# Unmixed weight blocks fetched raw, split at first use and written back once, with five plain half-experts

## The chip, the cores and the metric

The kernel runs on one core of a Trainium2 chip. The metric is the device time of one execution in microseconds (us). Besides the plain runs there is one profiled execution, whose trace gives all the rows below. TensorE (PE) multiplies, VectorE (DVE), ScalarE (ACT) and GpSimd (POOL) work on the results and on the weights, and SyncE (SP) issues nearly all DMA transfers.

## The reference

Three steps are chained: attention with a window of 64 positions over 32 heads of 576 positions, a dense layer pair with ELU, and eight experts whose outputs are weighted by a matrix P that is normalised by rows and columns in eight rounds. The change touches the last one alone:

```python
N, D, E, F = (2304, 512, 8, 1024)
...
out = np.zeros((N, D), dtype=np.float32)
for e in range(E):
    h = np.maximum(x @ w1[e], 0.0)
    ye = h @ w2[e]
    out += P[:, e:e + 1] * ye
```

## The kernel before, in words

Every float32 operand is split in two parts: a high part, rounded to the type that TensorE multiplies fast (`R32`), and a low part, the rest. A product of two operands is three matmuls: high by high, high by low, low by high. ScalarE makes the high part with a copy, and VectorE or GpSimd makes the low part with a subtraction.

The 2304 tokens are three groups of 768. An expert's 1024 hidden features are two **half-experts** of 512, so there are 16. A half-expert can be done in two ways.

- **Plain** (`e_in`, `e_out`, matmul lines L932 to L934 and L950 to L952): the first `PU` half-experts of group 0 run so, in units, with the weights' high and low parts held in SBUF as `forms` (tiles f). One unit has 96 matmuls of the first layer, half of them 512 and half 256 columns wide, and 72 of the second with 512 columns.
- **Block products** (`l1` and `l2`): all others, in **periods** of one half-expert each. Operands are cut into 2 x 2 blocks, and seven products of blocks, or of sums of blocks, take the place of eight. A period has 14 calls of `l1` (seven products for each of two halves p, six matmuls of 384 columns each, L1127) and seven calls of `l2` (18 matmuls of 256 columns in group 0, L1272, and 12 of 384 in the others, L1207). The loop goes in steps s of two `l1` calls and one `l2` call. `l2` follows `LAG` = 8 steps behind, so the first steps have `l1` calls alone.

A block product needs seven weight blocks of each matrix, split in high and low: three that are blocks of the matrix itself (*unmixed*; slots 0 to 2, products 1, 2 and 4 by `SLA` and 1, 2 and 3 by `SLB`) and four sums of blocks (slots 3 to 6). They are computed once and stored to DRAM (`wd1`, `wd2`; w1f and w2f are the tiles that fetch them). There are 64 matrices h to prepare (8 experts, 4 pieces, 2 layers), by four ways:

- `N1` of them during the dense layer, by `q_tasks`;
- the next `N3` at the dense layer's last stage, by `p_tasks`; `quiet` names all that no plain unit uses;
- those of the plain units, with some quiet ones among them, at due times that follow the count of plain steps (`due`, `clock`);
- the last ones, `tail`, by `late_tasks`: one task a call of `l1` from step 6 on, in the first periods.

In `p_tasks`, GpSimd makes the four sums (`p_sums`, tiles sw), ScalarE the high parts (`p_high`), VectorE the low ones (`p_low`), and SP stores them (`p_store`): part 1 is the sums (tiles g), part 0 the unmixed blocks (tiles f).

Each engine works through its instructions in the order in which they are written, and SP issues its transfers in such an order too. `w1_load` runs `NW1` calls ahead of `l1` and `w2_load` up to `NW2` products ahead of `l2`; a load waits on SP until the tile that it fills is free. In a call of `l1`, ScalarE moves results out of the PSUM banks la (tiles a, u, v), VectorE adds those of the banks lb to them (tiles c), and later the hidden forms (tiles h) are split: `hid` on ScalarE, then `hid_low` on VectorE for those with relu and on GpSimd for the others. What a call's product 4 leaves to do (`rest`, the add c<-lb,u and what hangs on it) is put in the list `late` and runs at the end of the step. There are two lb banks.

## Time and profile before

| | |
|---|---|
| median of 3 runs | 1964.22 us (1964.12 to 1965.58) |
| profiled execution, its time | 1965.19 us |
| its span, from first to last instruction | 1963.4 us |
| TensorE busy | 1948.9 us, 99% |
| VectorE / ScalarE / GpSimd busy | 1509.2 / 860.4 / 732.0 us |
| DMA moved | 495.17 MB, mean 252 GB/s |
| mean granted TensorE clock | 0.999 of full speed |

An engine is busy while one of its instructions executes; waiting for a semaphore is not busy. The plain units stand between about 499 and 809 us of the span, the block products of group 0 from 809 to about 1035, and those of groups 1 and 2 behind them.

### The profile page before, as it was taken

To read this page: it belongs to the slowest core of one execution; us is meant where nothing else is said; L and a number is where in the kernel's file an instruction comes from. 1 tells how busy PE (TensorE), PEld (TensorE's weight loads), DVE (VectorE), ACT (ScalarE), POOL (GpSimd) and SP (SyncE) were. 2 spreads that over 40 slices of the span, in tenths; PEclk is the share of its full clock that TensorE was granted. 3 is DMA by queue.
4 is the path that set the end of the run, shared out by engine and by line. 5 is a ranking of instruction groups with operands and counts; after the bars stand their busy time and mean duration, and the time that the engine had idled before them with its cause. 6 is when DMAs were issued, how large, how long until landed. Compare 5 with 4: busy or idle time off the path is not lost.

```text
span 1963.4 us, 33821 instructions
## 1 busy us (share of the span) xinstructions
PE 1948.9 (99%) x11898; PEld 1818.1 (93%) x11898; DVE 1509.2 (77%) x2567; ACT 860.4 (44%) x1821; POOL 732.0 (37%) x718
## 2 busy tenths in 40 slices
PE   8999999999999999999999999999999999999999
PEld 6888888898888888999999999999999999999998
DVE  6756676767797655687787888888887888888886
ACT  8885555555543433444343333333334333333332
POOL 4523232334355553443343333233253333232231
PEclk9999999999999999999999999999999999999999
DMA  9742354469799999699778777788888887777783
GB/s 205 191 93 56 107 173 151 153 219 323 274 377 378 378 361 340 235 360 340 242 249 310 259 260 263 240 275 259 293 263 253 256 271 263 261 261 260 235 280 118
DMA packets 311191, 495.17 MB, mean 252 GB/s; under 512 B 80352, under 2 KB 162416, under 8 KB 307312
## 3 DMA queue, kind: packets, MB, share of 16 engines
q1 hardware_dynamic: 309840, 492.73, 76.2%
q8 instruction: 95, 1.56, 0.3%
q14 instruction: 72, 0.59, 0.1%
q10 hardware_dynamic: 1184, 0.30, 0.1%
HBM read 361.78 MB, written 126.95 MB: 249 GB/s over the span
## 4 chain that ended last, share of the span: by engine, by line
PE 95%; ACT 3%; DVE 2%; DMA 0%; issue 0%; SPq 0%; DVEq 0%; ACTq 0%
PE la L1127 16%; PE lb L1127 12%; PE oa L1207 12%; PE ob L1207 11%; PE ob L1272 3%; PE oa L1272 3%; PE p L932 3%; PE p L933 3%; PE p L934 3%; PE ac L950 3%; PE ac L951 3%; PE p L213 3%; PE p L212 3%; PE ac L547 3%; PE ac L548 3%; PE ac L549 3%
## 5 line engine op out<-in xcount | busy, mean ns | idle before, releaser
L1109 POOL TENSOR_TENSOR h<-s,h 128x384 fp32r<-128x384 f32 x312 | 363.7, 1181 | 725.6 <-ACT h L1100 700.3
L1127 PE MATMUL la<-xf,w1f 128*128 128x384 f32 x1872 | 369.6, 335 | 1.4 <-ACT u L1147 1.3
L1127 PEld LDWEIGHTS la<-xf,w1f 128*128 128x128 f32 x1872 | 326.4, 188 | 2.6 <-ACT u L1147 2.1
L1127 PE MATMUL lb<-xf,w1f 128*128 128x384 f32 x1404 | 281.1, 334 | 0.0
L1100 ACT ACTIVATE h<-s 128x384 fp32r<-128x384 f32 x312 | 159.2, 522 | 246.8 <-DVE s L1151 239.8
L1207 PE MATMUL ob<-h,w2f 128*128 128x384 f32 x1344 | 252.3, 335 | 0.0
L1207 PE MATMUL oa<-h,w2f 128*128 128x384 f32 x1344 | 252.0, 335 | 0.2 <-DVE acc L1224 0.2
L1127 PEld LDWEIGHTS lb<-xf,w1f 128*128 128x128 f32 x1404 | 246.1, 188 | 0.0
L1207 PEld LDWEIGHTS oa<-h,w2f 128*128 128x128 f32 x1344 | 234.4, 188 | 0.5 <-DVE acc L1224 0.5
L1207 PEld LDWEIGHTS ob<-h,w2f 128*128 128x128 f32 x1344 | 234.4, 188 | 0.1
L1105 DVE SCALAR_TENSOR_TENSOR h<-c,h 128x384 fp32r<-128x384 f32 x234 | 193.0, 835 | 32.2 <-ACT h L1100 31.4
L1100 ACT ACTIVATE h<-c 128x384 fp32r<-128x384 f32 x234 | 122.8, 525 | 176.0 <-DVE c L1137 161.8
L739 POOL TENSOR_TENSOR sw<-rw 128x256 f32<-128x256 f32 x104 | 94.8, 912 | 183.8 <-DVE g L775 110.9
L1137 DVE TENSOR_TENSOR c<-c,pb 128x384 f32<-128x384 f32 x192 | 144.5, 752 | 6.6
L1224 DVE TENSOR_TENSOR acc<-ob,acc 128x768 f32<-128x768 f32 (+1 forms) x114 | 105.0, 924 | 37.4 <-PE ob L1207 37.4
L1224 DVE TENSOR_TENSOR acc<-oa,acc 128x768 f32<-128x768 f32 (+1 forms) x110 | 101.2, 923 | 37.3 <-PE oa L1207 37.3
L1151 DVE SCALAR_TENSOR_TENSOR s<-c,s 128x384 f32<-128x384 f32 x156 | 109.7, 703 | 13.4 <-DMA out_dram<-ost 2.4
L1147 ACT ACTIVATE v<-la 128x384 f32<-128x384 f32 x78 | 38.3, 491 | 162.0 <-PE la L1127 161.9
L254 ACT ACTIVATE hh<-p 128x512 fp32r<-128x512 f32 (+1 forms) x72 | 35.3, 490 | 161.9 <-PE p L934 161.7
L932 PE MATMUL p<-xh,f 128*128 128x256 f32 (+1 forms) x288 | 97.8, 339 | 0.0
L933 PE MATMUL p<-xl,f 128*128 128x256 f32 (+1 forms) x288 | 96.9, 336 | 0.0
L934 PE MATMUL p<-xh,f 128*128 128x256 f32 (+1 forms) x288 | 96.9, 336 | 0.0
(176 smaller groups left out, 3895.4 us busy)
## 6 DMA issues: line engine op xcount, KB each, us to landing
w1f<-wdi SPq DMA_DIRECT2D x546, 256.0 KB, 3.9
w2f<-wdo SPq DMA_DIRECT2D x273, 512.0 KB, 4.1
rw<-in_moe_w_dram SPq DMA_DIRECT2D x208, 128.0 KB, 4.8
wdi<-g SPq DMA_DIRECT2D x26, 1024.0 KB, 7.0
wdo<-g SPq DMA_DIRECT2D x26, 1024.0 KB, 7.4
wdi<-f SPq DMA_DIRECT2D x26, 768.0 KB, 5.1
wdo<-f SPq DMA_DIRECT2D x26, 768.0 KB, 5.3
raw<-in_moe_w_in_dram SPq DMA_DIRECT2D x16, 512.0 KB, 4.2
```

Source lines behind the costliest of these rows:

```text
L932: nc.tensor.matmul(p1[:, :n], w[:, s, 0, cs], xh, start=(c == 0), stop=False)
L933: nc.tensor.matmul(p1[:, :n], w[:, s, 0, cs], xl, start=False, stop=False)
L934: nc.tensor.matmul(p1[:, :n], w[:, s, 1, cs], xh, start=False, stop=(c == NCC - 1))
L1100: nc.scalar.activation(h[:, 0], src, AF.Relu if relu else AF.Copy)
L1105: nc.vector.scalar_tensor_tensor(h[:, 1], src, 0.0, r(h[:, 0]), op0=ALU.max, op1=ALU.subtract)
L1109: nc.gpsimd.tensor_tensor(out=h[:, 1], in0=src, in1=r(h[:, 0]), op=ALU.subtract)
L1127: nc.tensor.matmul(o, w[:, a, c, :], x[:, b, c, :], start=first and c == 0 and z == 0, stop=last and c == 1 and z == 2, skip_group_check=True,
L1137: nc.vector.tensor_tensor(out=t, in0=t, in1=pb[g, e][:, i], op=ALU.mult)
L1151: nc.vector.scalar_tensor_tensor(d[nm], d[a], 0.0, d[b], op0=ALU.max, op1=op)
L1207: nc.tensor.matmul(o[:, c], w[:, p, b, c * P:(c + 1) * P], hs[p][:, a, :], start=fresh and p == 0 and z == 0, stop=False, skip_group_check ...
L1224: nc.vector.tensor_tensor(out=a, in0=src, in1=a, op=ALU.add)
L1272: nc.tensor.matmul(o[:, c * HB2:(c + 1) * HB2], hs[p][:, a, c * P:(c + 1) * P], w[:, p, b, :], start=fresh and c != 1 and p == 0 and z == ...
```

## The change

Plain half-experts are five, not nine; four more half-experts of group 0 are block products, which makes 11 periods in group 0 where there were seven. The unmixed blocks are stored by no preparation any more. In group 0, and in group 1 for the half-experts that were plain in group 0, `w1_load` and `w2_load` fetch an unmixed block raw from the weights (tiles r, 128 KB in place of 256, and 256 in place of 512), `w_part` splits it into the tile that TensorE reads, and `w_back` writes that tile to DRAM once. `w_part` runs four `l1` calls, or two steps, ahead of the use; its low part is GpSimd's for the first layer, VectorE's for the second in group 0 and GpSimd's in group 1. `w_back` is issued one call (or one step) ahead of the use. The preparation's numbers change with it: `N1` and `N3` are 13, the tail is the eight matrices of the last expert, and the tile counts `NW1` and `NW2` are 9 and 6.

```diff
-    PU, N1, N3 = 9, 9, 9
-    tail = [(E - 1) * 2 * NP + i for i in (5, 6, 7)]
+    PU, N1, N3, LATE = 5, 13, 13, 8
+    tail = list(range(E * 2 * NP - LATE, E * 2 * NP))
...
+    mids = [[]]
+    for u in range(1, PU):
+        mids.append(rest[len(rest) * (u - 1) // (PU - 1):len(rest) * u // (PU - 1)])
     for u in range(PU):
         hs = [(4 * u + i, 4 + (4 * u + i - 4) % 8 if u else i) for i in range(4)]
-        if u >= 2 and rest:
-            hs.insert(1, (rest.pop(0), u % 4))
+        for i, h in enumerate(mids[u]):
+            hs.insert(2 * i + 1, (h, None))
...
-        if part:
-            nc.sync.dma_start(out=to[:, 3:7], in_=r(sums.pop(h)))
-        else:
-            nc.sync.dma_start(out=to[:, 0:3], in_=r(forms[h][:, 0:3]))
+        nc.sync.dma_start(out=to[:, 3:7], in_=r(sums.pop(h)))
...
             return load, [
-                lambda: high(0, 2), lambda: (low(0, 2), high(3, 1)), lambda: low(3, 1), sums,
-                *[nothing] * 2, lambda: high(4, 2), lambda: (low(4, 2), high(6, 2)),
-                lambda: low(6, 2), *[nothing] * 3,
+                sums, *[nothing] * 2, lambda: high(4, 2), lambda: (low(4, 2), high(6, 2)),
+                lambda: low(6, 2), *[nothing] * 2,
             ]
...
-    NW1, NW2, LAG = 12, 7, 8
+    NW1, NW2, LAG = 9, 6, 8
...
+    def raw_at(k, s):
+        g, e, pp = periods[k]
+        return s < 3 and (g == 0 or (g == 1 and 2 * e + pp < PU))
+
+    def w_part(key):
+        if key not in apart:
+            return
+        a, hi, lo, t, to, g = apart.pop(key)
+        nc.scalar.activation(hi, a, AF.Copy)
+        sub = nc.gpsimd if key[0] == 1 else (nc.vector, nc.gpsimd)[g]
+        sub.tensor_tensor(out=lo, in0=a, in1=r(hi), op=ALU.subtract)
+        back[key] = (to, t)
+
+    def w_back(key):
+        if key in back:
+            to, t = back.pop(key)
+            nc.sync.dma_start(out=to, in_=t)
...
+        if raw_at(k, s):
+            f, d = [fd for fd, v in PURE[0].items() if v == s][0]
+            f0 = f * (FF // 2) + (2 * pp + p) * P
+            a = P2["w1p"].tile([P, 2, P], F32, tag="r1", bufs=4, name="r1")
+            nc.sync.dma_start(
+                out=a,
+                in_=w1[e][d * 2 * P:(d + 1) * 2 * P, f0:f0 + P].rearrange("(c p) f -> p c f", p=P),
+            )
+            apart[1, n] = (a, t[:, 0], t[:, 1], r(t).rearrange("p z c f -> p z (c f)"), to, g)
+        else:
+            nc.sync.dma_start(out=r(t).rearrange("p z c f -> p z (c f)"), in_=to)
...
+        for n in range(4):
+            w_part((1, n))
+        w_back((1, 0))
...
                     w1_load(s * 2 + z + NW1)
+                    w_part((1, s * 2 + z + 4))
+                    w_back((1, s * 2 + z + 1))
...
+            ahead = 0 if s == 3 else s - LAG + 2
+            if s == 3 or ahead > 0:
+                w_part((2, ahead))
+            w_back((2, 0 if s == 4 else s - LAG + 1))
             while late:
                 late.pop(0)()
```

VectorE at the start of the first period, from call 4's c<-lb,v on. Tiles c, s and h are results and hidden forms of `l1`, r_7838 is the raw block of the second layer. Before:

```order
L1167 TENSOR_TENSOR c_8974<-lb,v 128x384
L1105 SCALAR_TENSOR_TENSOR h_8987<-c_8974,h_8987 128x384
L1151 SCALAR_TENSOR_TENSOR s_9002<-c_8938,r_9000 128x384
L1151 SCALAR_TENSOR_TENSOR s_9004<-c_8974,r_9000 128x384
L1151 SCALAR_TENSOR_TENSOR s_9006<-c_8938,s_9004 128x384
L1141 TENSOR_TENSOR c_9024<-lb,u 128x384
L1151 SCALAR_TENSOR_TENSOR s_9026<-c_9024,s_9006 128x384
L1141 TENSOR_TENSOR c_9037<-lb,a 128x384
```

The same place with the change:

```order
L1201 TENSOR_TENSOR c_7814<-lb,v 128x384
L1139 SCALAR_TENSOR_TENSOR h_7831<-c_7814,h_7831 128x384
L1185 SCALAR_TENSOR_TENSOR s_7848<-c_7776,r_7846 128x384
L1185 SCALAR_TENSOR_TENSOR s_7850<-c_7814,r_7846 128x384
L1185 SCALAR_TENSOR_TENSOR s_7852<-c_7776,s_7850 128x384
L1064 TENSOR_TENSOR w2f<-r_7838,w2f 128x2x256
L1175 TENSOR_TENSOR c_7875<-lb,u 128x384
L1185 SCALAR_TENSOR_TENSOR s_7877<-c_7875,s_7852 128x384
L1175 TENSOR_TENSOR c_7888<-lb,a 128x384
```

The split w2f<-r_7838 now stands ahead of the add c<-lb,u.

SP from the first loads of the loop (`w1_load(NW1)`) on, that is, the transfers issued while the first steps run. Before (the row with x6 holds the last four of the 12 loads made in advance and the first two of the loop):

```order
L1068 DMA w1f<-wdi_3_134 128x512 x6
L1068 DMA w1f<-wdi_0_135 128x512 x2
L1079 DMA w2f<-wdo_1_156 128x1024
L1068 DMA w1f<-wdi_0_135 128x512 x2
L1079 DMA w2f<-wdo_1_156 128x1024
```

With the change (the first row is the last load made in advance):

```order
L1086 DMA r_7510<-in_moe_w_dram 128x2x128
L1070 DMA wdi_2_125<-w1f 128x512
L1092 DMA w1f<-wdi_3_126 128x512
L1070 DMA wdi_2_125<-w1f 128x512
L1092 DMA w1f<-wdi_3_126 128x512 x3
L1086 DMA r_7817<-in_moe_w_dram 128x2x128
L1070 DMA wdi_3_126<-w1f 128x512
L1086 DMA r_7835<-in_moe_w_dram 128x2x128
L1107 DMA r_7838<-in_moe_w_dram 128x2x256
L1086 DMA r_7855<-in_moe_w_dram 128x2x128
```

The first fetch for `l2`, w2f<-wdo before and r_7838 now, stood behind four loads of the loop (calls 12 to 15) and stands behind six (calls 9 to 14) and three write-backs, each load with a tile that a call of `l1` sets free.

GpSimd from the last activation forms (xf) on. Before:

```order
L1025 TENSOR_TENSOR xf_8829<-xb_8653,xf_8829 128x768
L1025 TENSOR_TENSOR xf_8832<-xb_8646,xf_8832 128x768
L1109 TENSOR_TENSOR h_9016<-s_9002,h_9016 128x384
L1109 TENSOR_TENSOR h_9019<-s_9006,h_9019 128x384
L1109 TENSOR_TENSOR h_9039<-s_9004,h_9039 128x384
```

With the change:

```order
L1017 TENSOR_TENSOR xf_7661<-xb_7486,xf_7661 128x768
L1017 TENSOR_TENSOR xf_7664<-xb_7479,xf_7664 128x768
L1064 TENSOR_TENSOR w1f<-r_7490,w1f 128x256
L1064 TENSOR_TENSOR w1f<-r_7493,w1f 128x256
L1064 TENSOR_TENSOR w1f<-r_7502,w1f 128x256
L1064 TENSOR_TENSOR w1f<-r_7507,w1f 128x256
L1064 TENSOR_TENSOR w1f<-r_7510,w1f 128x256
L1143 TENSOR_TENSOR h_7864<-s_7848,h_7864 128x384
```

Five splits of raw blocks (calls 0, 1, 5, 7 and 8) stand between the activation forms and the first hidden form.

## Rows read from the trace of the kernel before

**Rows 1.** The page, busy us of each engine.
```profile
PE 1948.9 (99%) x11898; PEld 1818.1 (93%) x11898; DVE 1509.2 (77%) x2567; ACT 860.4 (44%) x1821; POOL 732.0 (37%) x718
```
**Rows 2.** Windows: five plain units, four group-0 periods; stretch, us, busy (instructions), clock, DMA.
```profile
core 0: us, PE busy (x) PEld busy (x) DVE busy (x) ACT busy (x) POOL busy (x), PEclk, DMA share, GB/s
641.37:806.56 165.19, 165.19 (x842) 141.42 (x841) 97.94 (x121) 62.92 (x89) 83.68 (x87) 1.00 0.94 338
882.46:1001.00 118.54, 118.54 (x843) 118.54 (x841) 91.94 (x177) 46.14 (x96) 48.89 (x41) 1.00 0.86 293
```
**Rows 3.** The page's groups: GpSimd's sums; count, busy us, mean ns, idle before.
```profile
L739 POOL TENSOR_TENSOR sw<-rw 128x256 f32<-128x256 f32 x104 | 94.8, 912 | 183.8 <-DVE g L775 110.9
```
**Rows 4.** Timeline of GpSimd, last activation forms: start us, us.
```profile
803.14 3.64 POOL L1025 TENSOR_TENSOR xf<-xb,xf 128x768 fp32r<-128x768 f32 x2
```
**Rows 5.** Timeline of TensorE, first period: calls 0 and 10.
```profile
809.27 1.23 PE L1127 MATMUL la<-xf,w1f 128*128 128x384 f32 x6
...
819.70 1.21 PE L1127 MATMUL lb<-xf,w1f 128*128 128x384 f32 x6
```
**Rows 6.** Groups by form, 853 to 912 us: GpSimd's late sums, ScalarE's late copies.
```profile
L843 POOL TENSOR_TENSOR qw<-qw 128x256 f32<-128x256 f32 x8 | 6.2, 770 | 3.5 <-DVE qf L823 1.8 <-ACT a L1147 1.3
...
L819 ACT ACTIVATE qf<-qw 128x512 fp32r<-128x512 f32 x6 | 3.7, 620 | 0.0
...
L819 ACT ACTIVATE qf<-qw 128x256 fp32r<-128x256 f32 x2 | 0.8, 405 | 0.0
```
**Rows 7.** Timeline of VectorE, first and second period.
```profile
813.56 0.56 DVE L1105 SCALAR_TENSOR_TENSOR h<-c,h 128x384 fp32r<-128x384 f32 x1 [1.35 <-ACT h L1100]
...
818.84 0.55 DVE L1141 TENSOR_TENSOR c<-lb,u 128x384 f32<-128x384 f32 x1
...
820.61 2.19 DVE L1105 SCALAR_TENSOR_TENSOR h<-c,h 128x384 fp32r<-128x384 f32 x2
...
847.65 0.68 DVE L823 TENSOR_TENSOR qf<-qw,qf 128x512 fp32r<-128x512 f32 x1
```
**Rows 8.** Timeline of SP's queue, first fetch for the second layer.
```profile
814.24 0.42 SPq L1079 DMA_DIRECT2D w2f<-wdo  x1
```
**Rows 9.** Tiles w1f, then w2f, 809 to 853 us: issue to landing.
```profile
DMA to landing us min/median/max: 2.8/5.6/7.9
...
DMA to landing us min/median/max: 4.9/6.0/7.9
```
**Rows 10.** Groups by form, VectorE, 853 to 912 us: late splits.
```profile
L823 DVE TENSOR_TENSOR qf<-qw,qf 128x512 fp32r<-128x512 f32 x7 | 7.3, 1036 | 0.0
...
L823 DVE TENSOR_TENSOR qf<-qw,qf 128x256 fp32r<-128x256 f32 x2 | 1.4, 684 | 0.0
```
**Rows 11.** Timeline of GpSimd, second period.
```profile
838.93 2.53 POOL L1109 TENSOR_TENSOR h<-s,h 128x384 fp32r<-128x384 f32 x2 [6.21 <-ACT h L1100]
...
844.97 2.30 POOL L1109 TENSOR_TENSOR h<-s,h 128x384 fp32r<-128x384 f32 x2
```
**Rows 12.** Timeline of TensorE, second period: two calls, four calls apart.
```profile
841.18 1.20 PE L1127 MATMUL la<-xf,w1f 128*128 128x384 f32 x6
...
849.65 1.20 PE L1127 MATMUL lb<-xf,w1f 128*128 128x384 f32 x6
```
**Rows 13.** DMA issues: count, KB each, median us to landing.
```profile
w1f<-wdi SPq DMA_DIRECT2D x546, 256.0 KB, 3.9
w2f<-wdo SPq DMA_DIRECT2D x273, 512.0 KB, 4.1
...
qw<-in_moe_w_dram SPq DMA_DIRECT2D x48, 128.0 KB, 3.8
wdi<-qf SPq DMA_DIRECT2D x12, 512.0 KB, 3.6
```
**Rows 14.** Windows: plain units, start of the periods, periods with late matrices.
```profile
574.00:641.00 67.00, 67.00 (x345) 57.03 (x344) 53.93 (x90) 26.44 (x38) 36.19 (x42) 1.00 1.04 378
...
810.00:826.00 16.00, 15.81 (x96) 15.45 (x95) 9.60 (x17) 7.11 (x16) 5.17 (x4) 1.00 0.86 298
...
853.00:912.00 59.00, 59.00 (x420) 59.00 (x420) 48.83 (x92) 24.52 (x52) 24.98 (x24) 1.00 0.99 358
```

More of the change, by code (lines that the diff above doesn't have):

```diff
@@ L760, in p_high @@
     def p_high(h, part):
-        n = 3 if part == 0 and h in quiet else 4
         b = slot_of[h]
@@ L768, in p_high @@
         src = (sws if part else rws)[h]
-        nc.scalar.activation(t[:, :n, 0, :], src[:, :n], AF.Copy)
+        nc.scalar.activation(t[:, :, 0, :], src, AF.Copy)
     def p_low(h, part):
-        n = 3 if part == 0 and h in quiet else 4
         t = (sums if part else forms)[h]
@@ L826, in low @@
             )
-            if a >= 4:
-                nc.sync.dma_start(out=to[:, a - 1:a + 1], in_=r(t))
-            else:
-                for i in range(n):
-                    s = [s for s in pos if pos[s] == a + i][0]
-                    nc.sync.dma_start(out=to[:, s], in_=r(t[:, i]))
+            nc.sync.dma_start(out=to[:, a - 1:a + 1], in_=r(t))
         def sums():
@@ L849, in q_tasks @@
             return load, [
-                lambda: high(0, 2), lambda: (low(0, 2), high(3, 1)), lambda: low(3, 1), sums,
-                *[nothing] * 2, lambda: high(4, 2), lambda: (low(4, 2), high(6, 2)),
-                lambda: low(6, 2), *[nothing] * 3,
+                sums, *[nothing] * 2, lambda: high(4, 2), lambda: (low(4, 2), high(6, 2)),
+                lambda: low(6, 2), *[nothing] * 2,
             ]
         return [
-            load, *[nothing] * 2, lambda: high(0, 2), lambda: (low(0, 2), high(3, 1)),
-            lambda: low(3, 1), sums, lambda: high(4, 2),
+            load, nothing, sums, nothing, lambda: high(4, 2),
             lambda: (low(4, 2), high(6, 2)), lambda: low(6, 2),
@@ L876, in begin @@
             p_sums(h, 0)
-            if n:
-                p_store(before, 0)
         def more():
             p_sums(h, 1)
+            if h in quiet:
+                rws.pop(h)
             if n:
@@ L889, in highs @@
         def highs():
-            p_high(h, 0)
+            if h not in quiet:
+                p_high(h, 0)
             if n:
-                p_store(before, 1)
+                p_store(before)
         def last():
-            p_low(h, 0)
+            if h not in quiet:
+                p_low(h, 0)
             p_load(n + 3)
@@ L1059 @@
     w1t, w2t = {}, {}
+    apart, back = {}, {}
+    def raw_at(k, s):
[13 more added lines that the diff above has]
+            nc.sync.dma_start(out=to, in_=t)
     def w1_load(n):
@@ L1067, in w1_load @@
         t = P2["w1p"].tile([P, 2, 2, P], R32, tag="w1", bufs=NW1, name="w1f")
-        nc.sync.dma_start(
-            out=r(t).rearrange("p z c f -> p z (c f)"), in_=wd1[e][2 * pp + p][:, SLA[pi]]
-        )
+        s = SLA[pi]
+        to = wd1[e][2 * pp + p][:, s]
+        if raw_at(k, s):
[9 more added lines that the diff above has]
+            nc.sync.dma_start(out=r(t).rearrange("p z c f -> p z (c f)"), in_=to)
         w1t[n] = t
@@ L1078, in w2_load @@
         t = P2["w2p"].tile([P, 2, 2, HB2], R32, tag="w2", bufs=NW2, name="w2f")
-        nc.sync.dma_start(out=r(t), in_=wd2[e][pp][:, SLB[out_order[x]]])
+        s = SLB[out_order[x]]
+        to = wd2[e][pp][:, s]
+        if raw_at(k, s):
+            f, d = [fd for fd, v in PURE[1].items() if v == s][0]
+            f0 = f * (FF // 2) + 2 * pp * P
+            a = P2["w2p"].tile([P, 2, HB2], F32, tag="r2", bufs=3, name="r2")
+            nc.sync.dma_start(
+                out=a,
+                in_=w2[e][f0:f0 + 2 * P, d * HB2:(d + 1) * HB2].rearrange("(q p) d -> p q d", p=P),
+            )
+            apart[2, n] = (a, t[:, :, 0], t[:, :, 1], r(t), to, g)
+        else:
+            nc.sync.dma_start(out=r(t), in_=to)
         w2t[n] = t
@@ L1490 @@
                 elif su > 2:
-                    while ntask < min(5 * NPRE + 3, 3.4 * (su - 2)):
+                    while ntask < min(5 * NPRE + 3, 4.6 * (su - 2)):
                         ptasks.pop(0)()
@@ L1505 @@
         for u in range(1, PU):
-            n = 5 if 0 <= u - 2 < len(others) - N1 - N3 else 4
+            n = 4 + len(mids[u])
             due += [12.0 * (u - 1 + (i + 1) / (5 * n)) for i in range(5 * n)]
```

9 lines of the change are left out of this document (4 added, 5 removed).

## The prediction

> **What bounds the kernel now.** I read the busy table first, then cut the span into stretches, then looked inside the stretches that the change touches. TensorE is busy 1948.9 of 1963.4 us [rows 1], so time goes down only where it gets less to do, and every new wait of TensorE is paid in full. The stretches [rows 2] give the price of the two ways to do a half-expert for group 0. The first holds five plain half-experts (each 96 matmuls of the first layer and 72 of the second, 840 together; the rest of the count straddles the edges): 165.19 / 5 = 33.04 us each. The second holds four block-product periods of group 0 (84 + 126 matmuls each, 840 again): 118.54 / 4 = 29.63 us each. In both TensorE is busy for the whole stretch at the full clock, so nothing else sets the pace there.
>
> **What is removed.** Four half-experts of group 0 move from plain to block products: 4 x (33.04 - 29.63) = **13.6 us** less TensorE work. No other matmul changes. That is the whole gain, since DMA, DVE and ACT work saved elsewhere lies under a TensorE that is already full.
>
> **Preparation, before the block products.** A unit of 33.04 us now prepares 6.5 weight matrices on average (4 plain, 2.5 others), not 5. GpSimd's sums grow by 1.5 x 4 x 0.91 us [rows 3] = 5.5 us on 83.68 / 5 = 16.7 us of 33 [rows 2], which is hidden. DVE has 97.94 of 165.19 us there, and gets about 1.5 more splits of the sums and 0.75 fewer of the raw blocks: hidden. The DMA gets lighter, since matrices that are not plain no longer store their three unmixed blocks as forms. The last unit's hand-over is close but fits: GpSimd ends the last activation form at 806.78 and TensorE starts the first block product at 809.27 [rows 4, 5]. Two block splits of 0.77 us [rows 6] now stand in that gap of 2.49 us. I count 0; if GpSimd came 1 us later it would cost that 1 us once.
>
> **The first period: a wait that is new.** Here the first layer runs alone, a call (six matmuls) each 1.04 us: call 0 starts at 809.27 and call 10 at 819.70 [rows 5]. In the order of the change, DVE's split of the first second-layer block stands ahead of the add that empties a PSUM bank of call 3 (c<-lb,u), and two lb banks exist, so call 10 needs that add. Before, it ran from 818.84 to 819.39 [rows 7], 0.3 us ahead of call 10. Now the fetch of that block is issued two steps into the period, behind loads whose buffer is free only when call 5 is done (809.27 + 6 x 1.04 = 815.5), about 816.3 with its own issue (before: 814.24 [rows 8]). It lands 5 us later (w1f and w2f: 2.8 to 7.9, medians 5.6 and 6.0, for blocks of its size and twice it [rows 9]): 821.3; ACT 0.62 us [rows 6]; DVE 0.7 to 1.04 (128x512 split: 0.68 alone, 1.04 mean [rows 6, 10]); the add 0.55: 823.4 or so, against 819.70. That is **3.7 us**, from 1.0 (landing in 2.8) to 6.8 (in 7.9). ACT stands in the same queue, so hidden-layer forms come late too, which mostly lies inside the same stall. A GpSimd split placed four calls ahead (4.2 us without the second layer) can be a little late once more, at the start of the second period; I take **4 us** for the start in all, 1 to 7.
>
> **The periods after it: four calls ahead.** Each period gets six splits on GpSimd (128x256: 0.77 us) and, in group 0, three on DVE. A GpSimd split for call n+4 is queued at call n. GpSimd's worst place in the trace: behind the call that starts at 841.18 its queue ends at 847.27, 6.1 us later, and four calls later starts at 849.65, 8.5 us later [rows 11, 12]. 6.1 + 0.8 = 6.9 us: it fits by 1.6 us. The write-back waits on SP for that split, and behind it stand loads that are needed eight calls (17 us) later, so a us there is hidden. ACT gets 6 x 0.4 + 3 x 0.62 = 4.3 us a period on 46.14 / 4 = 11.5 of 29.63, hidden. Cost 0; without this cover a late split would cost its lateness in each of 16 raw periods (11 in group 0, 5 in group 1).
>
> **The eight late matrices: where it gets tight.** They are prepared during about five periods (70 tasks, one a call), 148 us. DMA [rows 13]: a period fetched 14 x 256 + 7 x 512 = 7168 KB. Now it fetches 5632 KB and writes back 3072 KB: 301 GB/s at 29.63 us. A late matrix is 4 x 128 + 2 x 512 = 1536 KB in 8 calls, 2688 KB a period: 394 GB/s together. The same count for before gives 341 where the row says 358 [rows 14], so it is no overestimate. The most that any stretch moved is 378 GB/s at a share of 1.04, and 358 at 0.99 [rows 14]. Against 378 the excess is 4%, 6 us over 148; against 358 / 0.99 = 362 it is 9%, 13 us. Of this the prefetch absorbs some: a raw block is issued four calls, 8.5 us, ahead of its split's place in the queues and eight calls, 17 us, ahead of its use; landings take 5 to 6 [rows 9], so I count a backlog of 6 us as free. Cost 0 to 7. DVE there, in the stretch from 853: 48.83 us less the late splits of before, 7.3 + 1.4, leaves 40.1 of 59 [rows 10, 14], 20.1 us a period; three block splits and 3.5 late splits at 0.68 to 1.04 add 4.4 to 6.8: 83 to 91%. I take **2.5 us** for this stage, near the lower end, as the stretch at 0.99 [rows 14] cost TensorE nothing, with 0 to 9 as bounds.
>
> A row on sharing: DVE's two h splits from 820.61 took 1.09 us each while GpSimd worked, and the one at 813.56 took 0.56 while it was idle [rows 7]. The Trainium skill ("SBUF — State Buffer", Who interferes with whom) says that a DVE instruction with two SBUF inputs and a GpSimd instruction that reads SBUF lock each other out for a whole instruction. The trace agrees (1.09 against 0.56 us). By that rule up to 6 x 0.77 + 0.58 x 4 x 0.77 = 6.4 us a period of new GpSimd work could block DVE, which takes its 91% over 100% and would make the late stage 3 us dearer; by the rows' means alone it stays below.
>
> **Sum.** 1963.4 - 13.6 + 4 + 2.5 = 1956.3 us of span. The profiled execution took 1965.2, 1.0 above the median of the runs, 1964.22; from the median: **1957.1 us**. A measurement of this kernel tells about 0.2%, 3.9 us, from no change.
>
> **The rivals.**
> - All waits are hidden: the raw fetch lands in 3 us, and the DMA carries 394 GB/s. 1964.2 - 13.6 = 1950.6. For it: in the 16 us from 810, the tightest place so far, TensorE idled 0.2 us [rows 14]. Chance 0.27.
> - My forecast, some 2 to 9 us given back: 0.43.
> - The late stage is bound by DMA (or DVE): 13 us of deficit less 6 of slack, and a start of 6: 1964.2 - 13.6 + 13 = 1963.6, no difference. For it: 394 is above every row. Against: slack, and landings of 5 us at a share of 0.99. The skill's page "DMA: Bandwidth & Descriptors" (Where 436 GB/s comes from) gives about 358 GB/s as what HBM lets a core have, which would be this case; the row with 378 GB/s over 67 us speaks against it. Chance 0.20.
> - Slower: GpSimd's splits come late in each raw period. Price: each us beyond the 1.6 us of margin is paid 16 times. From 0.7 us beyond, 11 us, it decides: 1957.1 + 11 = 1968; at 1 us 1973. For it: new sums, splits and locks all fall on GpSimd's queue. Against: ahead of its worst place GpSimd idled 6.2 us [rows 11]. Chance 0.10.
>
> **How the numbers follow.** Faster 0.27 + 0.43 = 0.70; same 0.20; slower 0.10. The range goes from the case with all hidden to that of the late stage bound, 1950.5 to 1964.5; above it stand the slower case and some of the third.
>
> **What would show it.** Five plain units of 33.0 and eleven group-0 periods of 29.6 us show the gain. In the first period, TensorE idle of 3 to 4 us before call 10 and released by DVE's add (or the first second-layer product) shows the start. In periods two to six, a DMA share at or above 1.0, landings of 6 to 10 us, and TensorE idle released by ACT, GpSimd or DVE show the late stage; full TensorE there makes me wrong by 2.5 us. Gaps of equal size once in each raw period, up to group 1's fifth half-expert, would be the slower rival.

## The result, and the profile after

The change makes the kernel slower: 1989.34 us median of 4 runs (1987.95 to 1991.47) against 1964.9 of the kernel before beside it. The ratio is 1.0125, with a 95% interval of 1.0107 to 1.0142. The forecast was 1957.1 us, so 32 us were lost that it did not count. The stretches below are read from one profiled execution of each kernel; the change's took 1988.82 us.

The page, busy us of each engine, beside [rows 1]:

```profile
PE 1943.3 (98%) x12066; PEld 1824.3 (92%) x12066; DVE 1569.7 (79%) x2661; ACT 903.7 (45%) x1974; POOL 875.0 (44%) x861
```

The span is 1987.0 us. TensorE's idle time, span less busy, went from 14.5 to 43.7 us; its busy time fell by only 5.6, although there is 13.6 us less to do. Of the 8.0 between them some 4.6 us, an estimate from the 4.23 and 4.97 us that it was busy at half the clock (last section), went with the clock; in the periods with waits the same matmuls also count as busy for longer (121.1 us in periods 2 to 5, where four full periods take 118.5). To see where, the stretches are laid side by side, each from the first matmul of a unit or period to that of the next (us). Period 11 (7 before) is the first of group 1, and in the one behind it the first second-layer product of group 1 begins.

| | before | after | lost |
|---|---|---|---|
| plain units | 39.4, 35.0, 34.6, 33.0 (x5), 35.8 | 39.4, 38.7, 43.2, 33.8, 35.8 | 13.1 |
| periods 0, 1 | 17.3, 26.2 | 19.4, 26.8 | 2.7 |
| periods 2 to 5 | 29.6 each | 34.0, 31.4, 32.0, 32.5 | 11.5 |
| periods 6 to 10 | 29.6 (6, the last of group 0) | 29.6 each | 0 |
| change of groups | 29.6, 29.2 | 34.0, 35.7 | 10.9 |

The losses are 38.2 us. Less the 13.6 of four half-experts this is 24.6, and the spans differ by 23.6 (0.5 of the rest was gained ahead of and behind these stretches, the other half is rounding). The gain is there to the tenth: 29.6 in place of 33.0, four times. Three places eat it.

**Plain units.** The chain of waits from 538 to 625 us: who waited for whom, us in total, times, longest. The last two lines are from the kernel before, 538 to 608 us, its waits and its window (stretch, us, then the busy us of PE, PEld, DVE, ACT and POOL, granted clock, DMA share, GB/s).

```profile
ACT g L771 <- POOL sw L742: 29.6, 12, 5.2
...
POOL sw L742 <- DVE g L776: 13.8, 6, 4.0
PEld csum L640 <- DVE cs L636: 10.0, 5, 6.4
PE csum L640 <- DVE cs L636: 7.8, 4, 5.9
...
ACT g L769 <- POOL sw L739: 8.2, 3, 4.0
...
538.00:608.00 70.00, 70.00 (x361) 58.97 (x361) 65.76 (x126) 29.12 (x41) 41.46 (x46) 1.00 1.04 376
```

Before, TensorE was busy 70.00 of 70 there. The longest of these waits, as a timeline in the order of time:

```profile
579.27 1.42 DVE L776 TENSOR_TENSOR g<-sw,g 128x1024 fp32r<-128x1024 f32 x1
579.69 1.60 POOL L742 TENSOR_TENSOR sw<-sw,rw 128x256 f32<-128x256 f32 x1
...
581.25 0.72 POOL L742 TENSOR_TENSOR sw<-rw 128x256 f32<-128x256 f32 x1
581.93 0.72 POOL L742 TENSOR_TENSOR sw<-rw,sw 128x256 f32<-128x256 f32 x1
...
582.69 1.06 ACT L771 ACTIVATE g<-sw 128x1024 fp32r<-128x1024 f32 x1 [5.21 <-POOL sw L742]
...
583.65 0.37 ACT L254 ACTIVATE hh<-p 128x256 fp32r<-128x256 f32 x1
...
584.05 0.42 DVE L255 SCALAR_TENSOR_TENSOR hl<-p,hh 128x256 fp32r<-128x256 f32 x1 [3.35 <-ACT hh L254]
...
587.37 0.60 PE L640 MATMUL csum<-cs,ones 128*128 128x8 f32 x2 [5.94 <-DVE cs L636]
```

It is read from the bottom. TensorE stands for 5.94 us at the small product of P's rounds, whose VectorE steps come after hl. VectorE waits for ScalarE's hh (work of the plain product itself). ScalarE has stood 5.21 us at a copy of the sums, which GpSimd has not finished. So work that nobody is in a hurry for (g) stands ahead of work that TensorE waits for (hh), in one queue. GpSimd in its turn waited 13.8 us for VectorE's g, which frees one of its two buffers for sums. TensorE's stand goes with the lower clock: windows, with the same columns.

```profile
585.20:591.60 6.40, 4.23 (x11) 3.46 (x12) 6.09 (x14) 2.25 (x3) 3.25 (x4) 0.50 0.91 320
592.00:610.00 18.00, 17.72 (x86) 14.62 (x86) 17.38 (x33) 6.20 (x8) 11.02 (x13) 1.00 0.80 262
```

**Periods 2 to 5.** Windows over them and over periods 6 to 10, then waits from 736 to 866 us:

```profile
736.00:770.00 34.00, 30.54 (x212) 29.71 (x211) 28.19 (x49) 16.10 (x36) 17.35 (x18) 1.00 1.03 366
770.00:801.40 31.40, 30.08 (x213) 29.73 (x212) 25.96 (x47) 15.83 (x36) 22.17 (x23) 1.00 1.01 357
801.40:833.40 32.00, 30.19 (x213) 29.67 (x212) 27.77 (x48) 14.32 (x33) 21.28 (x22) 1.00 1.03 368
833.40:865.90 32.50, 30.30 (x213) 29.66 (x212) 29.94 (x51) 16.37 (x36) 19.09 (x20) 1.00 0.99 351
865.90:1014.00 148.10, 148.10 (x1052) 148.10 (x1051) 118.55 (x227) 72.22 (x159) 77.31 (x74) 1.00 0.93 324
```
```profile
ACT w1f L1062 <- DMA wdi<-w1f: 18.0, 8, 5.2
POOL w1f L1064 <- ACT w1f L1062: 15.4, 6, 5.6
```

The DMA's share is 0.99 to 1.03 while the late matrices are made, and TensorE is full as soon as they are done. What ScalarE waits for is the write-back of the tile that its split fills again. In one case it was issued at 744.93 and landed at 751.35:

```profile
744.93 0.42 SPq L1070 DMA_DIRECT2D wdi<-w1f  x1
...
751.46 0.42 ACT L1062 ACTIVATE w1f<-r 128x256 fp32r<-128x256 f32 x1 [5.19 <-DMA wdi<-w1f]
```

Counted through the trace, this is the write-back of call 29 and the split of call 36. In the five longest of these waits the tile came round after seven calls, not after the nine of `NW1`, and the split stands four calls ahead of its use.

**The change of groups.** Windows 1014 to 1084 us, with the window of the kernel before (1001 to 1031 us) between them; VectorE's groups by form in the first, the two s rows of the kernel before (L1151) ahead of those of the change (L1185); and ScalarE's timeline in the second:

```profile
1014.00:1048.00 34.00, 30.62 (x212) 29.72 (x211) 32.89 (x53) 14.93 (x32) 18.66 (x16) 1.00 0.70 237
...
1001.00:1031.00 30.00, 30.00 (x215) 30.00 (x214) 28.76 (x51) 12.40 (x24) 11.93 (x10) 1.00 0.68 219
...
1048.00:1084.00 36.00, 32.11 (x178) 31.79 (x177) 26.44 (x40) 16.49 (x35) 20.03 (x19) 0.91 1.00 342
```
```profile
L1151 DVE SCALAR_TENSOR_TENSOR s<-c,s 128x384 f32<-128x384 f32 x4 | 3.1, 776 | 0.3
L1151 DVE SCALAR_TENSOR_TENSOR s<-c,r 128x384 f32<-128x384 f32 x4 | 2.1, 554 | 0.1
...
L1185 DVE SCALAR_TENSOR_TENSOR s<-c,s 128x384 f32<-128x384 f32 x4 | 4.6, 1156 | 0.3
L1185 DVE SCALAR_TENSOR_TENSOR s<-c,r 128x384 f32<-128x384 f32 x4 | 3.8, 966 | 0.1
...
L1064 DVE TENSOR_TENSOR w2f<-r,w2f 128x512 fp32r<-128x512 f32 x3 | 2.1, 704 | 0.0
```
```profile
1063.39 0.81 ACT L1256 ACTIVATE acc<-oa 128x768 f32<-128x768 f32 x1 [6.05 <-DMA out_dram<-acc]
1064.09 0.48 ACT L1181 ACTIVATE v<-la 128x384 f32<-128x384 f32 x1
```

VectorE is busy 32.89 of 34 us: this is where the next group's activations are summed and split, and it had 28.76 of 30 already before. GpSimd is busy 18.66 us in the stretch, 11.93 before. The second stall is a wait of ScalarE for an output store (issued late, at 1057.68, as SP had waited for VectorE's last sums); v, which TensorE needs, stands behind it.

### The profile page after: what moved, and what is told of

It reads as the page before. It is cut to its first block, busy times and chain, and to the rows that moved or that the text cites. A ratio compares the mean times of both kernels' runs of the same rounds, so it can differ in the third digit from the quotient of the medians.

```text
span 1987.0 us, 34682 instructions
## 1 busy us (share of the span) xinstructions
PE 1943.3 (98%) x12066; PEld 1824.3 (92%) x12066; DVE 1569.7 (79%) x2661; ACT 903.7 (45%) x1974; POOL 875.0 (44%) x861
## 4 chain that ended last, share of the span: by engine, by line
PE 76%; DVE 8%; DMA 8%; POOL 3%; issue 2%; ACT 2%; SPq 1%; DVEq 0%; ACTq 0%; POOLq 0%
PE la L1161 15%; PE oa L1241 11%; PE lb L1161 11%; PE ob L1241 11%; PE p L213 2%; PE p L212 2%; PE p L214 2%; PE ac L547 2%; PE ac L548 2%; PE ac L549 2%; PE oa L1306 2%; PE ob L1306 2%; POOL sw L742 2%; DMA wdi<-w1f 2%; DVE acc L1322 1%
## 5 line engine op out<-in xcount | busy, mean ns | idle before, releaser
L1143 POOL TENSOR_TENSOR h<-s,h 128x384 fp32r<-128x384 f32 x344 | 399.3, 1175 | 663.6 <-ACT h L1134 645.9
L1161 PE MATMUL la<-xf,w1f 128*128 128x384 f32 x2064 | 409.2, 336 | 8.5 <-ACT v L1181 5.7
L1161 PEld LDWEIGHTS la<-xf,w1f 128*128 128x128 f32 x2064 | 359.7, 188 | 11.2 <-ACT v L1181 6.4
L1161 PE MATMUL lb<-xf,w1f 128*128 128x384 f32 x1548 | 311.7, 336 | 11.3 <-DVE c L1175 6.0
L1161 PEld LDWEIGHTS lb<-xf,w1f 128*128 128x128 f32 x1548 | 271.6, 188 | 13.6 <-DVE c L1175 7.1
L1139 DVE SCALAR_TENSOR_TENSOR h<-c,h 128x384 fp32r<-128x384 f32 x258 | 213.8, 838 | 47.9 <-ACT h L1134 46.6
L1185 DVE SCALAR_TENSOR_TENSOR s<-c,s 128x384 f32<-128x384 f32 x172 | 126.6, 736 | 13.6 <-DMA out_dram<-ost 1.0
L1064 POOL TENSOR_TENSOR w1f<-r,w1f 128x256 fp32r<-128x256 f32 x96 | 82.5, 870 | 56.2 <-ACT w1f L1062 55.3
L836 POOL TENSOR_TENSOR qw<-qw 128x256 f32<-128x256 f32 x84 | 69.5, 828 | 76.3 <-DMA qw<-in_moe_w_dram 57.5
L1185 DVE SCALAR_TENSOR_TENSOR s<-c,r 128x384 f32<-128x384 f32 x172 | 96.7, 603 | 5.2 <-ACT r L1212 1.8
L235 DVE SCALAR_TENSOR_TENSOR m<-m,p 128x512 f32<-128x512 f32 (+1 forms) x78 | 50.1, 642 | 55.2 <-ACT m L247 54.9
```

The costliest lines, as they stand in the source:

```text
L836: nc.gpsimd.tensor_tensor(out=rw[:, o], in0=rw[:, a], in1=rw[:, b], op=op)
L1064: sub.tensor_tensor(out=lo, in0=a, in1=r(hi), op=ALU.subtract)
L1139: nc.vector.scalar_tensor_tensor(h[:, 1], src, 0.0, r(h[:, 0]), op0=ALU.max, op1=ALU.subtract)
L1143: nc.gpsimd.tensor_tensor(out=h[:, 1], in0=src, in1=r(h[:, 0]), op=ALU.subtract)
L1161: nc.tensor.matmul(o, w[:, a, c, :], x[:, b, c, :], start=first and c == 0 and z == 0, stop=last and c == 1 and z == 2, skip_group_check=True,
L1185: nc.vector.scalar_tensor_tensor(d[nm], d[a], 0.0, d[b], op0=ALU.max, op1=op)
```

## The experiments

The edits of e1 to e8 are against the changed kernel, those of e9 to e14 against the run that each names; long ones are shown in part. Lost us as in the table above, from the one profiled execution of each; "6 to 8" are periods. Time is the median; where a kernel was timed in rounds, the ratio to before has its interval, and the other rows but the first are single runs. The profiled execution of e10 took 1971.0 us, the most of its ten (1965.3 to 1971.0), so differences of 2 or 3 us between e10 to e13 in the periods from 2 on say nothing.

| run | time | dense layer | plain units | 0, 1 | 2 to 5 | 6 to 8 | change |
|---|---|---|---|---|---|---|---|
| the change | 1989.34 | 0 | 13.1 | 2.7 | 11.5 | 0 | 10.9 |
| e1_mid | 1989.11 | 0 | 13.3 | 5.9 | 7.6 | 0 | 10.4 |
| e2_no_late_stores | 1982.15 | 2 | 13.2 | 3.8 | 0.9 | 0 | 11.0 |
| e3_no_write_back | 1973.96 | 0 | 13.2 | 3.8 | 0.1 | 0 | 6.0 |
| e4_nine_plain | 1982.19, 1.0087 (1.0071 to 1.0104) | 1 | 0 | 3.1 | 4.4 | 0 | 10.3 |
| e5_no_sums | 1974.81 | 0 | 1.2 | 3.1 | 8.1 | 0 | 11.2 |
| e6_moved | 2063.29 | 90 | 0 | 4.1 | 0.9 | 6.1 | 10.7 |
| e7_no_out_stores | 1982.23 | 0 | 13.1 | 3.8 | 10.0 | 0 | 4.4 |
| e8_remedies | 1988.19, 1.0121 (1.0102 to 1.0140) | 21 | 4.3 | 3.8 | 0 | 0 | 7.6 |
| e9_spaced | 1976.96, 1.0058 (1.0041 to 1.0075) | 0 | 0.1 | 3.8 | 0.1 | 20.0 | 1.5 |
| e10_deadline | 1968.01, 1.0016 (1.0007 to 1.0026) | -1 | 0 | 3.9 | 1.6 | 14.7 | 1.3 |
| e11_order | 1966.71, 1.0011 (1.0002 to 1.0021) | 0 | 0 | 3.7 | 0.8 | 10.1 | 1.4 |
| e12_ten_calls | 1964.01, 0.9995 (0.9985 to 1.0004) | -1 | 0 | 3.2 | 3.3 | 7.3 | 1.5 |
| e13_gpsimd_low | 1965.34, 1.0002 (0.9992 to 1.0011) | -1 | 0.2 | 3.0 | 2.6 | 6.4 | 2.4 |
| e14_six_plain | 1960.00, 0.9979 (0.9970 to 0.9989) | -2 | 0 | 3.6 | 0.7 | 0 | 0.8 |

**e1_mid**: the quiet matrices of units 1 to 4, 2, 3, 2, 3 in the change, become 0, 0, 5, 5.
```diff
-        mids.append(rest[len(rest) * (u - 1) // (PU - 1):len(rest) * u // (PU - 1)])
+        mids.append(rest[len(rest) * max(0, u - 3) // 2:len(rest) * max(0, u - 2) // 2])
```


> Edit: the ten quiet matrices that stood among plain units 1 to 4 (2, 3, 2, 3) stand in units 3 and 4 alone (0, 0, 5, 5). Theory A (in units 1 and 2 GpSimd's sums come so densely that ScalarE, which waits for them in its queue, gives VectorE and the normalising rounds of P their inputs late): units 1 and 2 fall from 38.7 and 43.2 us to about 35, and no clock drop follows there; units 3 and 4 may rise by 0 to 4 us; in all 8 to 13 us faster than the change, some 1976 to 1981. Rival (the units are short of DMA, or of time to prepare five units at all): units 1 and 2 stay within 2 us of 38.7 and 43.2.

The 8 to 13 us did not come: the loss moves with the matrices, one unit ahead of where they are listed (39.4, 35.0, 39.7, 39.9, 37.1), and stays as large. P's rounds, which end in the third unit, are where it showed first, and not its cause.

**e2_no_late_stores**: `low` in the late tasks stores nothing; expert 7's block products read expert 6's blocks.
```diff
-            nc.sync.dma_start(out=to[:, a - 1:a + 1], in_=r(t))
+            if pre == "pre":
+                nc.sync.dma_start(out=to[:, a - 1:a + 1], in_=r(t))
```


> Edit: the eight late matrices are loaded, summed and split, but not stored (8 x 1024 KB less); expert 7's block products read expert 6's blocks, so the output of expert 7 is left out. Theory B1 (the first six periods lose 13.9 us because the DMA is full): periods 2 to 5 fall from 34.0, 31.4, 32.0, 32.5 to 29.6 to 30.2 us, DMA share under 0.92, 9 to 12 us faster. Theory B2 (GpSimd's and VectorE's added work is the cause, sums and splits of the late matrices): that work is all still there, so the periods keep at least 8 of the 11.8 us.

**e3_no_write_back**: `w_back` does nothing; later groups read a sum block's place.
```diff
-        if key in back:
-            to, t = back.pop(key)
-            nc.sync.dma_start(out=to, in_=t)
+        back.pop(key, None)
...
+            to = wd1[e][2 * pp + p][:, s + 3 if s < 3 else s]
```


> Edit: no split block is written back; where a later group would fetch it, it fetches a sum of blocks of the same matrix instead (as many bytes), so the output is left wrong for three blocks in seven. Theory B1: the write-backs (3072 KB a period, and the wait of ScalarE's split for the write-back that last used its tile) are what fills the DMA: periods 0 to 5 lose under 4 us instead of 13.9. Theory B2: they keep 10 or more. At the change of group: theory C (VectorE is full in the first period of group 1, which has nothing to do with write-backs, then ScalarE waits for an output store): the 34.0 us period stays above 33, the 35.7 us one falls to 29 to 31 if the store lands earlier. Rival: both fall to 29.2.

With either of the two streams away, periods 2 to 5 are full but for 0.9 and 0.1 us, though all splits on VectorE and GpSimd stay. So their loss is DMA traffic, not the engines. In e2 the DMA's share did not fall under 0.92 as expected: from 770 to 801 us it is 1.00 at 347 GB/s, and TensorE is busy 31.00 of 31.00. A full share alone thus costs nothing; what went with it is ScalarE's waits for write-backs, 1.5 us from 736 to 866 us in place of 18.0. Without write-backs the second stall at the change shrinks too (30.8 in place of 35.7); the first (34.0) stays.

**e4_nine_plain**: the new way of storing with the old counts.
```diff
-    PU, N1, N3, LATE = 5, 13, 13, 8
+    PU, N1, N3, LATE = 9, 9, 9, 3
```


> Edit: the new way to fetch, split and write back, with nine plain half-experts, nine matrices ahead in each of the first two stages and three late ones, as before. Theory A says that the plain units are as before (33 to 35 us each, 0 to 3 us lost), theory B that three late matrices cost 3 to 6 us with the start, theory C that the change of group costs 8 to 11: 1976 to 1985 us, slower than before. Rival (the loss comes from having five plain half-experts): 1963 to 1968, the same as before.

Without fewer plain units the new way costs 17.9 us (1982.19 against 1964.32 beside it): nothing in the plain units, but start, one late period and the change of groups as in the change. These losses belong to fetch and write-back, that of the plain units to the new counts: fewer units with more matrices each.

**e5_no_sums**: in `p_tasks` GpSimd makes no sums; ScalarE and VectorE split raw blocks in their place (three raw and two sum buffers become four raw ones).


> Edit: GpSimd makes no sums for the matrices prepared from the dense layer's last stage on; ScalarE and VectorE split the raw blocks in their place, so the stored sums are left out of the output. All copies, splits and transfers stay (one more raw buffer, no sum buffer). Theory A1 (GpSimd's sums are what ScalarE's queue waits for in the plain units): units 1 and 2 fall from 38.7 and 43.2 us to under 36 each, no clock drop there, and unit 3 to 33.0. Theory A2 (VectorE's or the DMA's own load): units 1 and 2 stay above 37 and 40. Periods unchanged, 34.0 and 35.7 us at the change of group among them.

The units take 39.4, 35.0, 35.8, 33.0 and 35.8 us, with VectorE's and ScalarE's splits all there. The plain units' loss is the wait for GpSimd's sums. Whether GpSimd's own time or its wait for a free sum buffer counts for more is not separated, as both are gone.

**e6_moved**: 23 matrices in the dense layer, none between the plain ones, late ones over 12 calls each.


> Four edits in separate stages: 23 matrices ahead in the dense layer, not 13, at 4.5 tasks a step, so none of the quiet ones stands among the plain units; the late matrices at 12 tasks each, not 8; the first raw block of the second layer fetched ahead of the first period; the second-layer splits of group 0's last period on GpSimd. Theory A: units 39.4, 35.0, 34.6, 33.0, 35.8 or less, if the dense layer has room (it shows before unit 0, at 499.0 us now). Theory B1 (DMA): with a third less late traffic a us, periods 2 to 5 lose under 4 us in all instead of 11.3. Start: period 0 falls from 19.4 to 17.3 to 17.8. Theory C: VectorE has 2.1 us less in the 34.0 us period, which falls to 30 to 32.5; if GpSimd's splits cost VectorE as much by contention, it stays at 33 to 34. Sum 1955 to 1966.

Plain units and periods 2 to 5 are mended, but the dense layer ends 90 us later: each matrix had to wait for the one raw buffer (from 254 to 488 us GpSimd waited 141.4 us in all for fetches of qw, and ScalarE 104.9 for its sums), and ScalarE's and VectorE's other work stood behind it. The first period at the change of groups takes 33.0 us, which is the expectation's alternative: with its splits on GpSimd, VectorE is still busy 31.82 of 33 us (from 1088 us), and s<-c,r takes 924 ns.

**e7_no_out_stores**: the four output stores of group 0 left out.


> The changed kernel without the four output stores of group 0 at its last period (these rows of the output are not written; everything else is as in the change). Theory: the second stall at the change of groups (first-layer period after it 35.7 us, ScalarE's copy into the accumulator waiting 6.05 us for the store out<-acc) is the store's landing behind a loaded SP queue and DMA; without the store that period takes about 30 to 31 us and the one before stays at 34.0, in all about 5 us less, 1984. Rival: VectorE and GpSimd are the bound in both periods and the store's wait only covers it: 34 and 34 to 35, time as in the change, 1988 to 1989.

The two periods take 34.0 and 29.2 us: the second stall is the store's landing, the first is not. (Periods 2 to 5 share out their loss otherwise from kernel to kernel: 32.8, 29.7, 31.2, 34.7 here.)

**e8_remedies**: four choices changed together; the core of it:
```diff
-    PU, N1, N3, LATE = 5, 13, 13, 8
+    PU, N1, N3, LATE = 5, 23, 13, 4
...
-        return s < 3 and (g == 0 or (g == 1 and 2 * e + pp < PU))
+        return s < 3 and g == 0
...
+        elif h not in quiet:
+            nc.sync.dma_start(out=to[:, 0:3], in_=r(forms[h][:, 0:3]))
```


> Five plain half-experts and raw fetches in group 0 as in the change, with four other choices: 23 matrices (not 13) are prepared in the dense layer, through two raw buffers and with the low parts written in place, so one other matrix per plain unit and four late ones, each over 12 calls; the plain units' unmixed blocks are stored as forms as before, so group 1 fetches nothing raw; in group 0's last period the second layer's raw splits are GpSimd's. Theory (the three losses come from GpSimd's and ScalarE's queue in the plain units, from DMA above its ceiling in the late periods, and from raw splits plus write-backs at the change of groups): plain units 39.4 35.0 34.6 33.0 36, late periods 29.6 to 30.5, change of groups 29.5 to 31.5 twice, start 2 us: 1964.9 - 13.6 + 2 + 2 to 6 = 1955 to 1961. Rival (raw fetch and write-back themselves do not fit even in group 0 alone, or the denser preparation starves the dense layer): 1965 to 1980.

All periods of group 0 from the third on take 29.6. The rival came true in the dense layer, 21 us: waits there, 250 to 450 us:

```profile
POOL qw L888 <- DMA qw<-in_moe_w_dram: 54.1, 18, 5.8
ACT gh L239 <- DVE m L235: 45.6, 29, 4.9
ACT qh L892 <- POOL qw L888: 34.6, 14, 4.2
```

The fetch was issued two steps ahead of the sums, on SP behind the store that frees its buffer.

**e9_spaced**: e8 with four steps a matrix, 18 in the dense layer and ten late; group 0's last period stored whole.
```diff
-        return s < 3 and g == 0
+        return s < 3 and g == 0 and (e, pp) != (E - 1, NP // 2 - 1)
```


> As the kernel with the four remedies, with the work laid out once more: 18 matrices in the dense layer at four steps each (raw block fetched three steps ahead of its sums, in place of two), 13 at its last stage, three others in the plain units (one each from the third unit on), ten late ones over 12 calls each; and the four matrices of group 0's last period are stored with all seven blocks, so that this period neither splits nor writes back. Theory (each loss is preparation on a full queue): the dense layer ends at 499 to 503 us as before; plain units 39.4 35.0 34.6 33.0 35.8; start 2 to 3 us; late periods 29.6; change of groups 29.2 and 29.1 as before, since VectorE and SP then have what they had there: 1964.2 - 13.6 + 2 to 5 = 1953 to 1956. Rivals: the change of groups costs 3 or more still (the lag comes from the raw periods before it): 1957 to 1960; ten late matrices bring back the DMA's backlog: 32 us in some periods, 1960 to 1965.

Dense layer, plain units, periods 2 to 5 and the change of groups (29.7, 30.6) are mended, the last with it: without raw splits and write-backs for group 0's last half-expert VectorE keeps up (28.89 of 30 us from 1011 us on). A new loss stands in periods 6 to 8: TensorE's longest wait from 800 to 1080 us, and what stands ahead of u, in the order of time:

```profile
PE la L1231 <- ACT u L1251: 9.7, 1, 9.7
...
916.86 3.17 POOL L841 TENSOR_TENSOR qw<-qw 128x256 f32<-128x256 f32 x4
...
924.27 3.13 POOL L841 TENSOR_TENSOR qw<-qw 128x256 f32<-128x256 f32 x4 [4.25 <-DMA qw<-in_moe_w_dram]
926.64 0.63 ACT L822 ACTIVATE qf<-qw 128x512 fp32r<-128x512 f32 x1 [5.95 <-POOL qw L841]
...
927.98 0.47 ACT L1251 ACTIVATE u<-la 128x384 f32<-128x384 f32 x1
```

It is the plain units' picture again: ScalarE's copies wait for GpSimd's sums, and u, which TensorE needs, stands behind them. The code says why it stands here. At the first step of period 8 the kernel gives the late matrices' buffers back, and runs all tasks that are left at once:

```python
if late_cm:
    while ltasks:
        ltasks.pop(0)()
```

The tasks start at call 12 and come one a call, so that 24 of the ten matrices' are left at call 114: the last two matrices, whose sums (916.86 and 924.27) have no call of `l1` between them.

**e10_deadline**: e9 with nine late matrices, 14 at the dense layer's last stage. **e11_order**: that, with
```diff
-            if s == 3 or ahead > 0:
+            if ahead > 0:
                 w_part((2, ahead))
...
             while late:
                 late.pop(0)()
+            if s == 3:
+                w_part((2, 0))
```


> As the spaced kernel, with nine late matrices and 14 at the dense layer's last stage in place of ten and 13. Theory: the spaced kernel's 19 us of waits in periods 6 to 8 (33.2, 33.5, 42.1 us) were the late matrices' due time: at 12 calls each the last of ten was stored at call 138, and its blocks are wanted from about call 120 on; with nine the last is stored at call 126 and wanted, for the second layer, from about 135 on. Then periods 6 to 8 take 29.6 to 30.5, everything else stays: 1976.96 - 19 + 0 to 3 = 1957 to 1961. Rival: those waits are DMA over its ceiling or a full queue, which nine meet as well: 33 us there again, 1968 to 1975.

> As the kernel with nine late matrices, with the start mended: the first raw block of the second layer is fetched before the loop, and its split stands behind the add c<-lb,u of the third step in VectorE's order, not ahead of it. Theory (TensorE's 2.0 us there, and the clock's half step behind it, are that order): first period 17.3 to 18 us in place of 20.5, all else as in the kernel beside it: 2.5 to 3.2 us less than that, 1954 to 1958. Rival: the wait only moves to the hidden forms, which come late too: first and second period together as before, no difference.

Of the 20.0 us in periods 6 to 8, 5.3 went with the tenth matrix. Neither theory alone explains the rest, but period 8 follows the tasks that are left at call 114: 42.1 us with 24 (e9), 35.8 and 34.4 with 12 (e10, e11), 29.6 with none (e12, e13). The order at the start takes 1.9 us off period 0 and gives 1.7 back in period 1: the rival was right, the wait moves on.

**e12_ten_calls** (e11 with the late tasks over 10 calls) and **e13_gpsimd_low** (that, with all raw splits' low parts on GpSimd):


> As the kernel with the start mended, with 10 calls for each of the nine late matrices in place of 12, so that the last one is stored at call 108 and not 126. Theory (what is left, 33.1, 31.4 and 34.4 us in periods 6 to 8, is still the due time, since behind a loaded queue the last stores come close to their use): 29.6 to 30.5 us in periods 6 to 8, the earlier periods at 29.6 to 30.5: 1966.7 - 10 + 0 to 4 = 1957 to 1961. Rival: it is VectorE's occupancy (26.6 of 30 us there) with late work on top, or the DMA's share: the same 10 us come in other periods: 1964 to 1970.

> As the kernel with 10 calls for each late matrix, with the raw second-layer blocks' low parts on GpSimd in place of VectorE in all of group 0 (some 2 to 4 us a period moved). If VectorE's occupancy sets the waits that are left, the late periods fall by 1 to 3 us each below those of the kernel beside it, and the first period by up to 1; if due times or DMA do, no difference within 2 us; if GpSimd's queue is the tighter one, each raw period of group 0 grows by 0.5 to 2 us, 5 to 15 in all.

With the tasks done by call 108 period 8 is full, but period 6 takes 36.8 us; periods 2 to 8 lose 10.6 us in all, where e11 lost 10.9. That is the rival, the same loss in other periods, though the median is 2.7 us lower. Moving VectorE's splits makes no difference. What is seen in e12, in windows and in waits from 820 to 905 us, is the change's late stage again, write-backs behind a full DMA:

```profile
805.00:835.00 30.00, 30.00 (x214) 30.00 (x213) 25.24 (x48) 14.99 (x36) 17.25 (x18) 1.00 1.02 363
835.00:865.00 30.00, 27.35 (x190) 26.82 (x189) 23.70 (x40) 12.62 (x29) 18.38 (x21) 1.00 1.03 359
```
```profile
ACT w1f L1132 <- DMA wdi<-w1f: 12.0, 5, 4.5
```

**e14_six_plain**: e11 with six plain half-experts and four late matrices.
```diff
-    PU, N1, N3, LATE = 5, 18, 14, 9
+    PU, N1, N3, LATE = 6, 18, 14, 4
```


> As the kernel with the start mended and 12 calls for each late matrix, with six plain half-experts in place of five and so four late matrices in place of nine. Theory (what is left in the kernels before is the late matrices' bytes, fetched and stored on top of the raw fetches and write-backs): three half-experts' gain, 3 x 3.41 = 10.2 us, start and second period 3 to 4, change of groups 2, late periods 29.6 to 29.8: 1964.4 - 10.2 + 5 to 7 = 1959 to 1961. Rival: raw periods lose some tenths each whatever the late work (GpSimd's and VectorE's queues), so that ten raw periods give 5 us back: 1963 to 1966, no difference.

```profile
787.00:817.00 30.00, 30.00 (x214) 30.00 (x213) 25.29 (x46) 13.78 (x31) 21.26 (x22) 1.00 1.04 383
817.00:847.00 30.00, 30.00 (x214) 30.00 (x213) 25.64 (x52) 16.54 (x37) 14.99 (x15) 1.00 1.03 375
```

From the fourth on no period of group 0 loses anything, and the kernel beats both: 1960.0 us, within the expected 1959 to 1961 and 0.2% below before. In e8, too, five plain half-experts with four late matrices lost nothing in these periods. So in e10 to e13 most of what was left came with the late matrices.

## Why the prediction was wrong

- **The gain, 13.6 us**: right. Units of 33.0 and periods of 29.6 us, four exchanged.
- **Preparation "hidden", 0 us: this step failed, by 13.1 us.** I compared each engine's busy sum with the length of a unit (GpSimd 16.7 of 33 us, plus 5.5) and took what fits for hidden. The means were those of the last five units, four of which the change removes; where the added matrices went, from 538 to 608 us, VectorE had 65.76 of 70 us and GpSimd 41.46 already before. The matrices of a unit are prepared as a chain, though (GpSimd's sums, ScalarE's copy, VectorE's subtraction), and the copy stands in ScalarE's queue ahead of hh. When GpSimd is a little behind, ScalarE waits, and the plain product with it. With the change GpSimd is busy 32.30 us of the 39 from 538 us on. e5 shows the wait, e1 that it follows the matrices. GpSimd is slowed there, too: the sum at 579.69 took 1.60 us beside VectorE's g, those after it 0.72. The Trainium skill ("SBUF — State Buffer", Who interferes with whom) has a reason for that: a VectorE instruction with two SBUF inputs contends with a GpSimd instruction that reads SBUF. The trace agrees in this place. No run separated this share.
- **The hand-over to the block products, 0**: right (35.8 us before and after).
- **The start, 4 us**: right mechanism, too large. TensorE idled 2.05 us at 700.44, ended by VectorE's add c<-lb,u behind the split w2f<-r, as forecast:

```profile
701.28 0.69 DVE L1064 TENSOR_TENSOR w2f<-r,w2f 128x512 fp32r<-128x512 f32 x1 [1.78 <-ACT w2f L1062]
...
701.89 0.55 DVE L1175 TENSOR_TENSOR c<-lb,u 128x384 f32<-128x384 f32 x1
...
702.49 0.81 PE L1161 MATMUL lb<-xf,w1f 128*128 128x384 f32 x3 [2.05 <-DVE c L1175]
```

  The fetch landed 5.2 us after its issue, near the 5 taken, but it was issued 5.5 us into the period (695.40) and not 7.0, so the wait was shorter. With period 1, 2.7 us. e11 shows that the order is not all: behind the add, the same time comes one period later.
- **Splits on GpSimd "four calls ahead", 0**: right; the rival that ended on the slower side did not come. Periods 6 to 10, all raw, take 29.6 us.
- **The late stage, 2.5 us: mis-sized, 11.5 measured.** The bound was in the working: 394 GB/s asked, 362 to be had by the more careful row, 13 us of deficit. What failed is the 6 us of backlog that I took for free because loads are issued early. A write-back must land before its tile is filled again, and a split that waits for it blocks ScalarE; that wait does not use the prefetch, and I had called the write-back's delay hidden. The third rival named this stage, at 13 less 6; e2 and e3 show that the traffic is its cause.
- **The change of groups: missing altogether, 10.9 us.** I looked at the edges of the old stages that the diff touches and not at the first period of group 1, where group 0's last second-layer products still run and VectorE already had 28.76 of 30 us. Three more splits (2.1 us), and GpSimd's at the same time, made it late by 4.4 us. VectorE's s<-c,r went from 554 to 966 ns. That is the place for the rule of the Trainium skill ("SBUF — State Buffer", Who interferes with whom) that I had weighed at the late stage. e6 took the three splits off VectorE and gained 1.0 us; e9 shows that the loss goes with that half-expert's splits and write-backs, once group 1's are gone (e8); the lock's own share was not separated. The second stall, 6.5 us, is the output store (e7), late through SP and the write-backs (e3).

My rivals had one place each. The result was three moderate losses at once, none of which alone is larger than the gain (13.1 against 13.6). The misses add up: 13.1 for the preparation, 10.9 for the change of groups, 9.0 more in the late stage and 1.3 less at the start are 31.7 of the 32.2 us. The slower side held 10%, by a mechanism that did not occur.

**What stays open**: why 3 to 4 us stay in the first two periods whatever the order, and what makes periods 2 to 6 of e12 lose 10.5 us, with nothing left over for period 8. One rival was not tested. SP's transfers share eight semaphores, and from 736 to 866 us 91 of 160 were issued within 0.3 us of the landing of the transfer before them on the same one (before, 853 to 912 us: 16 of 59). So the late stage may be held up by the number of transfers under way rather than by their bytes; e2 and e3 take away both.
